# Block products with fewer multiplications for the last quarter of a feed-forward's first matmul, with token and weight sums made on chip

## The chip, the cores and the metric

One core of one Trainium2 chip runs the whole program. The metric is the device time of one execution in microseconds. TensorE multiplies, VectorE (DVE), ScalarE (ACT) and GpSimd (POOL) do elementwise work, SyncE (SP) issues the loads.

## The reference

Three layers in a row, all in float32. The first is a linear recurrence over 768 steps for 2 batches of 8 heads of 48. Its result, 1536 tokens of 384, goes through a feed-forward with ELU, and that through four experts with ReLU, weighted by shares.

```python
x = attn_out.transpose(0, 2, 1, 3).reshape(1536, 384)
h = x @ w_in                                              # 384 -> 2048
g = np.where(h > 0.0, h, np.exp(np.minimum(h, 0.0)) - 1.0)
x = g @ w_out                                             # 2048 -> 384
p = domain_probs / (domain_probs.sum(-1, keepdims=True) + 1e-09)
for e in range(4):                                        # 384 -> 1024 -> 384 each
    out += p[:, e:e + 1] * (np.maximum(x @ w1[e], 0.0) @ w2[e])
```

## The kernel before

**Numbers.** A float32 operand is kept as a rounded high part and the rest, its low part, and a product is three matmuls (high by high, high by low, low by high) into one PSUM bank (`PASSES`). ScalarE makes high parts (`copy("A", ...)`, L192), VectorE or GpSimd low parts (`sub`, L188). Weights of the first feed-forward come as float64 words and are turned into both parts by `piece`: `wl` loads, `wa`, `wb` and `wc` convert (L219 to L261). Tokens are 3 blocks of 512, features 128 to a block; a matmul is 128x128 by 128x512.

**First feed-forward.** `step(n)` has n = 12 q + 4 bl + f: quarter q of the 2048 hidden features, token block bl, feature block f in the quarter. `h` is the hidden product, 9 matmuls (L478) and two activations for the ELU; `e` the rest of the ELU on VectorE (L486) and the high part; `el` the low part; `z` nine matmuls into three PSUM banks (L505), which collect four f; `dr` adds the banks into `x2` (L514), and in the last quarter splits the new x into high (ScalarE) and low (GpSimd).

**Second feed-forward, `experts`.** Two feature blocks by three token blocks by three parts of the inner dimension are a *unit*. The first two units are plain products (`plain`, L709: 36 of 3 matmuls, 12 banks, copied out by `plain_taken` on ScalarE). The other fourteen are made of 15 block products instead of 18 (`product`, L677): sums of token blocks (`sum_tokens`, L657, split by `tokens_hi` and `tokens_lo`, L660 to L667) by sums of weight blocks (`sum_blocks` on GpSimd, L595, split by `split_hi` and `split_lo`), collected in five chains of banks and drained by `taken` (L689 to L696: 10 on VectorE, 5 on ScalarE). `second` (L738) are the second products, of hidden low parts made at L731.

**What sets the order.** All is under a manual schedule: each engine runs its instructions in the order in which the program writes them. For attention and the first feed-forward that order is the string `ORDER`, tokens such as `h20`, `el20D` (step and engine: A ScalarE, D VectorE, P GpSimd). The part behind `|` overlaps with `experts`: each token gets a key that counts 3 for an h or a z and ends at -1 with the last, and the events of `experts` have keys in rows of one block product, row 0 being the first plain product.

```python
            n -= 3 * (token[0] in "hz")
...
            at(n - (75 if u > 2 else 112 if u == 2 else 95), load_blocks, u)
...
            at(made[t[0]], sum_tokens, t[0] in FIRST, *t)
```

So unit 2's blocks are loaded 70 rows ahead of row 0, summed from 55 and split from 40 rows ahead; the first 16 token sums have the keys -0.9 to 14.85, and the hidden low parts that the first second products read have 12.7 to 17.2. Buffers that matter: two for `blocks`, three for `sums` (split weights), two for `e`, three for `hl`, eight PSUM banks.

## Time and profile before

| | |
|---|---|
| median of 3 runs | 644.77 us (643.35 to 647.09) |
| the profiled execution's own time | 641.47 us |
| its span | 639.7 us |
| granted TensorE clock | 0.997 of full speed |
| TensorE busy | 627.2 us, 98% |
| VectorE busy | 485.2 us, 76% |
| GpSimd busy | 363.1 us, 57% |
| ScalarE busy | 302.0 us, 47% |

The span is the profiled execution from its first to its last instruction; the own time is a little longer. The profile and the runs are different executions. Line numbers (L677) are those of the kernel before.

### The profile page before, as it was taken

How to read it: one execution, taken by the hardware profiler on the slowest of the kernel's cores; microseconds unless marked ns; L12 is line 12 of the kernel's file. 1: busy time of each engine (PE TensorE's matmuls, PEld its weight loads, DVE VectorE, ACT ScalarE, POOL GpSimd, SP SyncE). 2: the span in 40 equal slices, each digit the busy share in tenths (PEclk: the TensorE clock that was granted, in tenths of full speed). 3: DMA queues.
4: the chain of work that ended last, by engine and by line, in shares of the span. 5: the costliest groups of instructions: out<-in, count | busy, mean ns of one | idle time of the engine just before them, and what ended most of it. 6: DMA issues, size and time to landing. Idle time of an engine off the chain costs nothing.

```text
span 639.7 us, 10184 instructions
## 1 busy us (share of the span) xinstructions
PE 627.2 (98%) x3858; PEld 513.2 (80%) x3858; DVE 485.2 (76%) x709; ACT 302.0 (47%) x587; POOL 363.1 (57%) x320
## 2 busy tenths in 40 slices
PE   9999999999999999999999999999999999999995
PEld 7777878788888888888888888888888888888884
DVE  7899995537759633598876987977978968878683
ACT  2666755456757636557434424433532434344230
POOL 6876465103232538648452876876876867754252
PEclk9999999999999999999999999999999999999998
DMA  8966640131231300003103112012220121400012
GB/s 317 344 225 206 209 167 9 46 123 50 75 99 37 138 1 0 1 0 115 51 18 108 41 34 91 26 45 81 70 79 18 41 75 33 124 1 1 0 50 105
DMA packets 20974, 52.07 MB, mean 81 GB/s; under 512 B 2680, under 2 KB 3880, under 8 KB 20916
## 3 DMA queue, kind: packets, MB, share of 16 engines
q1 hardware_dynamic: 20772, 51.33, 24.2%
q8 instruction: 32, 0.52, 0.4%
q14 instruction: 26, 0.21, 0.1%
q10 hardware_dynamic: 144, 0.00, 0.0%
HBM read 47.76 MB, written 2.38 MB: 78 GB/s over the span
## 4 chain that ended last, share of the span: by engine, by line
PE 90%; DVE 5%; DMA 3%; issue 1%; ACT 0%; SPq 0%; DVEq 0%; ACTq 0%
PE second L738 29%; PE bank L505 14%; PE bank L478 14%; PE chain_a L677 9%; PE chain_b L677 6%; PE chain_p L709 4%; PE chain_c L677 3%; PE chain_d L677 3%; DMA v<-in_vv 2%; PE chain_e L677 1%; PE bank L138 1%; DMA raw<-in_w_out 1%; PE bank L361 1%; PE bank L368 1%; DVE t L224 1%
## 5 line engine op out<-in xcount | busy, mean ns | idle before, releaser
L738 PE MATMUL second<-hl,w2s 128*128 128x512 f32 x864 | 230.8, 389 | 0.1
L738 PEld LDWEIGHTS second<-hl,w2s 128*128 128x128 f32 x864 | 162.0, 188 | 34.3 <-DVE hl L188 0.5
L756 POOL TENSOR_TENSOR x<-scaled,x 128x512 f32<-128x512 f32 x60 | 84.1, 1420 | 91.5 <-DVE scaled L748 91.3
L478 PE MATMUL bank<-x,w 128*128 128x512 f32 x432 | 105.1, 391 | 0.0
L505 PE MATMUL bank<-hl,w 128*128 128x512 f32 x432 | 104.8, 391 | 0.0
L731 DVE SCALAR_TENSOR_TENSOR hl<-terms,hl 128x512 fp32r<-128x512 f32 x92 | 95.1, 1046 | 11.0 <-ACT hl L725 11.0
L505 PEld LDWEIGHTS bank<-hl,w 128*128 128x128 f32 x432 | 80.7, 188 | 17.1 <-issue 0.3
L478 PEld LDWEIGHTS bank<-x,w 128*128 128x128 f32 x432 | 80.6, 188 | 17.1 <-issue 0.3
L188 POOL TENSOR_TENSOR sums<-blocks,sums 128x512 fp32r<-128x512 f32 (+1 forms) x56 | 74.8, 1345 | 26.9 <-ACT sums L192 26.9
L188 POOL TENSOR_TENSOR hl<-e,hl 128x512 fp32r<-128x512 f32 x26 | 35.6, 1372 | 74.0 <-ACT hl L192 74.0
L595 POOL TENSOR_TENSOR blocks<-blocks 128x256 f32<-128x256 f32 x84 | 73.5, 893 | 1.2 <-DMA blocks<-in_w 0.5
L486 DVE SCALAR_TENSOR_TENSOR e<-e,bank 128x512 f32<-128x512 f32 x48 | 32.6, 681 | 50.7 <-ACT e L482 50.7
L692 ACT ACTIVATE terms<-chain_b 128x512 f32<-128x512 f32 x28 | 16.8, 600 | 106.0 <-PE chain_b L677 106.0
L725 ACT ACTIVATE hl<-terms 128x512 fp32r<-128x512 f32 x96 | 58.1, 624 | 14.1 <-PE second L738 6.8
L692 ACT ACTIVATE terms<-chain_a 128x512 f32<-128x512 f32 x28 | 16.8, 598 | 77.3 <-PE chain_a L677 77.3
L481 ACT ACTIVATE e<-bank 128x512 f32<-128x512 f32 x48 | 28.6, 595 | 48.6 <-PE bank L478 45.5
L677 PE MATMUL chain_a<-x,sums 128*128 128x512 f32 x168 | 47.3, 390 | 0.0
L748 DVE TENSOR_TENSOR scaled<-second,pr 128x512 f32<-128x512 f32 x60 | 40.6, 686 | 2.7 <-PE second L738 1.4
L230 POOL TENSOR_TENSOR raw<-raw,t 128x384 int32<-128x384 int32 x21 | 22.2, 1063 | 31.6 <-ACT t L226 24.2
L689 DVE TENSOR_TENSOR terms<-terms,chain_a 128x512 f32<-128x512 f32 x42 | 28.7, 682 | 14.0 <-PE chain_a L677 13.4
L192 ACT ACTIVATE hl<-e 128x512 fp32r<-128x512 f32 x48 | 30.0, 627 | 15.8 <-DVE e L486 10.9
L677 PEld LDWEIGHTS chain_a<-x,sums 128*128 128x128 f32 x168 | 31.5, 188 | 6.9 <-DVE terms L689 0.4
(129 smaller groups left out, 966.9 us busy)
## 6 DMA issues: line engine op xcount, KB each, us to landing
v<-in_vv SPq DMA_DIRECT2D x12, 544.0 KB, 6.1
kr<-in_wkr SPq DMA_DIRECT2D x12, 512.0 KB, 5.7
raw<-in_w_out SPq DMA_DIRECT2D x16, 384.0 KB, 3.5
raw<-in_w_in SPq DMA_DIRECT2D x16, 384.0 KB, 4.5
blocks<-in_w SPq DMA_DIRECT2D x16, 384.0 KB, 3.3
raw<-in_w SPq DMA_DIRECT2D x16, 384.0 KB, 4.3
w<-in_wkr SPq DMA_DIRECT2D x12, 262.5 KB, 5.5
gw<-in_wkr SPq DMA_DIRECT2D x12, 262.0 KB, 2.8
```

Of the source, the lines that this page charges most:

```text
L188: engines[e].tensor_tensor(o, a, b.bitcast(F32), ALU.subtract)
L478: nc.tensor.matmul(ph, lhsT=wi[:, sa, f, kk, :], rhs=x[:, kk, c0:c0 + nch, sm], start=(kk == 0 and i == 0), stop=(kk == 2 and i == 2))
L486: nc.vector.scalar_tensor_tensor(b["e"], b["e"], -1.0, b["ph"], ALU.add, ALU.max)
L505: nc.tensor.matmul(pxs[q, bl][d][:, :cols], lhsT=wo[:, sa, f, d * P:(d + 1) * P], rhs=b["t"][:, sm], start=(f == 0 and i == 0), stop=(f == ...
L595: nc.gpsimd.tensor_tensor(*(places(blocks[u], p) for p in (r, a, c)), ALU.subtract if op == "-" else ALU.add)
L677: nc.tensor.matmul(banks[c], lhsT=weights(u, r, sa), rhs=tokens(r)[:, sm], start=r in HEADS and i == 0, stop=i == 2, skip_group_check=True)
L692: nc.scalar.activation(out=new({0: 0, 6: 5, 3: 2, 5: 3, 8: 4}[r]), in_=ps, func=AF.Copy, scale=-1.0 if r in (6, 8) else 1.0)
L725: nc.scalar.activation(out=hls[f, b][:, 0], in_=results[f, b], func=AF.Copy if weighted else AF.Relu)
L731: nc.vector.scalar_tensor_tensor(hls[f, b][:, 1], results[f, b], 0.0, hls[f, b][:, 0].bitcast(F32), ALU.max, ALU.subtract)
L738: nc.tensor.matmul(sums[d], lhsT=w[:, sa, f, d * P:(d + 1) * P], rhs=hls[4 * h + f, b][:, sm], start=f == i == 0, stop=f == 3 and i == 2)
L748: nc.vector.tensor_tensor(o, sums[d], prs[h // 2, b], ALU.mult)
L756: nc.gpsimd.tensor_tensor(x2[:, d, s], scaled[d], x2[:, d, s], ALU.add)
```

## The change

The last quarter's hidden products (h36 to h47) are made by two more units of 15 block products, numbered -2 and -1, inside the lead. Products are tokens p0 to p29 and their drains k0 to k29. The quarter's weights are laid out as blocks; `wb12` to `wb15` round into the `blocks` buffers, and `sb` (sums) and `sp` (splits) make the operands. Token blocks are put together again from high and low part and summed by 25 `pt` tokens, split by 12 `tf` tokens into places of x that are no longer read. `x` starts the ELU from a finished sum in SBUF (two activations), `y` is the rest of it on VectorE, then `e`, `el` and `z` as before; five of the z are cut in three (`za`, `zb`, `zc`). Results of unit -2 lie in the quarter's weight buffer, those of unit -1 among the eight `first` buffers, which are now handed out one by one. Because units -2 and -1 use the two `blocks` buffers, loads and splits of units 0 and 1 and of unit 2's first part move to tokens (`mb`, `mu`, `ms`) near the end of the order, with unit 2's sums on VectorE instead of GpSimd.

```diff
+GROUPS = {"h": 3, "z": 3, "za": 1, "zb": 1, "zc": 1, "p": 1}
...
+PARTS = [((1, 1), None, None), ((2, 1), None, None), ("q", (1, 1), (2, 1)), ((1, 0), None, None), (8, (1, 0), (1, 1)),
+         ((2, 0), None, None), ("s2", (2, 0), (2, 1)), ("v", 8, "s2"), (12, 8, (2, 1)), ((0, 1), None, None),
...
+z7 e18 e17 el18P z16 dr7A h19 xd11 | el17D pt3D pt12D pt0D pt9D pt1D pt13P z17 e19 h8 pt5D pt4D pt6D z18 el19D pt2P
+pt8D pt14P tf8P e8 tf12D h11 e11 z19 el8D dr19D h9 e9 el11D pt10P h10 wl8 z8 pt11D el9D e10 el10D pt7P tf11D h20 wl9
+z9 wa9D wa8D e20 h21 wb9D wl11 wb8D pt15D el20D wa11D wc9D z10 pt19D h22 wl10 z11 wc8P e21 wl24 wa10D e22 wb11D wl25
+wb10D el22D wc11D tf1D el21D wc10D pt22D wl27 tf0D dr11A h23 wl26 wa24D z20 pt16P h24 e23 wb24D wa25D z21 el23D wc24D
+pt21D e24 wb25P h25 z22 pt17D wa27D wl12 el24D e25 h27 wb27P wa26D el25D wc25P wb26P z23 wl13 e27 dr23D h26 pt20P
+wa12D z24 el27D wc26P e26 wa13D h28 z25 tf4P el26D wb12D wl15 wb13D h29 wc27D e28 sb0D z26 e29 el28D h30 z27 wl28 wl14
+pt23D el29D wa15D e30 wl29 wb15D dr27D sb1P tf7P el30D h32 z28 sp0D h31 wa14D wb14P tf10P z29 pt18D e32 e31 wl31 p0
+z30 k0 p1 el31D tf13D sb2D k1 p2 k2 sp1D h33 p3 el32D z31 k3 p4 pt24P tf9P e33 k4 el33D tf5D h34 p5 wa28D k5 e34 h35
+sb3P p6 dr31D wb28P k6 p7 tf2D mb0 z32 el34P k7 p8 k8 wl30 sp2P p9 k9 x36 za33 p10 e35 p11 zb33 zc33 k10 k11 wa30D p12
+k12 y36 p13 p14 x37 wa29D p15 e36 p16 za34 k13 k14 p17 el35D k15 k16 k17 zb34 y37 wc28P x40 sp3P wb29D el36D p18 p19
+wa31D wb30D k18 k19 zc34 p20 za35 y40 p21 k20 wc29P k21 zb35 zc35 p22 p23 e37 e40 dr35D k22 wb31P za36 k23 p24 el40P
+x41 k24 p25 zb36 k25 p26 x38 y41 el37P p27 wc30P k26 zc36 mb1 y38 p28 wc31P za37 k27 k28 x39 e38 y39 x45 zb37 zc37 e39
+z40 el38D x42 e41 y45 el39D z38 y42 el41P x44 z39 x43 y44 z41 e44 y43 p29 x46 el44P e42 el42P e45 dr39D z44 y46 el45D
+e46 z42 k29 el46D x47 e43 el43D y47 z45 e47 z46 el47D mu0D z43 mb2 ms2D mu1D z47 mu2P dr43D dr47D
...
+            if key == 3 and fifteen:
+                u = q // 2 - 2
+                if u not in blocks:
+                    blocks[u] = pools["blocks"].tile([P, 17, P], F32, tag="blocks", name="blocks")
+                at = 6 + 3 * (q % 2)
+                engines[e].tensor_tensor(blocks[u][:, at:at + 3].rearrange("q b c -> q (b c)").bitcast(I32), hi, b["t"], ALU.add)
+                return
...
+        def summed():
+            b["ph"] = results[f - 4, bl]
+            started()
+
+        def joined():
+            nc.vector.scalar_tensor_tensor(b["ph"], b["e"], -1.0, b["ph"], ALU.add, ALU.max)
+            b["e"] = b["ph"]
...
+            if (f - 4, bl) in held:
+                released((f - 4, bl))
...
-        def sum_blocks(u, r, a, op, c):
-            nc.gpsimd.tensor_tensor(*(places(blocks[u], p) for p in (r, a, c)), ALU.subtract if op == "-" else ALU.add)
+        def sum_blocks(u, r, a, op, c, e="P"):
+            engines[e].tensor_tensor(*(places(blocks[u], p) for p in (r, a, c)), ALU.subtract if op == "-" else ALU.add)
...
+        def sum_parts(e, name, a, c):
+            t = full["m", name] = kept(("m", name))
+            if a is None:
+                k, i = name
+                hi, lo = (x[:, k, 4 * i:4 * i + 4, m].bitcast(F32) for m in range(2))
+                engines[e].tensor_tensor(t.rearrange("q (n c) -> q n c", n=4), hi, lo, ALU.add)
+            else:
+                engines[e].tensor_tensor(t, full["m", a], full["m", c], ALU.add)
+                used(("m", a), ("m", c))
...
-                results[2 * u + o // 3, o % 3] = term()
+                f, b = 2 * u + o // 3, o % 3
+                results[f, b] = term() if u >= 0 else kept((f, b)) if u == -1 else wt64[3].rearrange(
+                    "p s (n c) -> p (s n) c", c=512)[:, o].bitcast(F32)
...
-            n -= 3 * (token[0] in "hz")
+            n -= GROUPS.get(token.rstrip("0123456789"), 0)
...
+        def sum_tokens_of(n, e):
+            sum_parts(e, *PARTS[n])
+
+        def split_tokens(r, e):
+            tokens_hi(r, ("m", r))
+            tokens_lo(e, r, ("m", r))
+
+        def sum_weights(n, e):
+            for t in SUMS[3 * (n % 2):3 * (n % 2) + 3]:
+                sum_blocks(n // 2 - 2, *t, e)
+
+        def split_weights(u, part, e):
+            for i in (0, 4):
+                m = min(4, 8 - part - i)
+                split_hi(u, part, (9, 0)[part], 8 - part, i, m)
+                split_lo(e, u, part, (9, 0)[part], 8 - part, i, m)
+
+        def split_first(u, e):
+            if u == 2:
+                return split_weights(u, 0, e)
+            for i in (0, 3):
+                split_hi(u, 0, 6, 6, i, 3)
+                split_lo(e, u, 0, 6, 6, i, 3)
+
+        def sum_first(u, e):
+            for t in SUMS:
+                sum_blocks(u, *t, e)
+
+        if lead:
+            fifteen.update(p=lambda n: product(n // 15 - 2, TURNS[n % 15]), k=lambda n: taken(n // 15 - 2, TURNS[n % 15]), pt=sum_tokens_of,
+                           tf=split_tokens, sb=sum_weights, sp=lambda n, e: split_weights(n // 2 - 2, n % 2, e), mb=load_blocks,
+                           mu=split_first, ms=sum_first)
         for u in range(16):
             n = place["product", u, 0] if u > 1 else -90 + 12 * u
+            if lead and u < 3:
+                if u == 2:
+                    for i in (0, 4):
+                        at(n - 10 + i, split_hi, u, 1, 0, 7, i, min(4, 7 - i))
+                        at(n - 8.6 + i, split_lo, "P", u, 1, 0, 7, i, min(4, 7 - i))
+                continue
```

Before the bar the order is the same. The host also lays out the last quarter of `w_in` by blocks; the loads keep their sizes. The tail of the order before reads `e46 h47 el46P dr43D z44 e47 el47D z45 z46 z47 dr47D`.

## Rows read from the trace of the kernel before

**Rows 1.** The page's totals: busy us (share of the span) and instructions of each engine.
```profile
PE 627.2 (98%) x3858; PEld 513.2 (80%) x3858; DVE 485.2 (76%) x709; ACT 302.0 (47%) x587; POOL 363.1 (57%) x320
```

**Rows 2.** The chain that ended last, in order: start us, us, what.
```profile
260.55 8.16 PE bank L505 x36
268.71 24.48 PE chain_p L709 x108
```

**Rows 3.** Windows by stage: length, then busy us of each engine, clock, DMA.
```profile
132.03:200.00 67.97, 67.97 (x301) 56.30 (x301) 43.83 (x76) 44.61 (x80) 17.99 (x16) 1.00 0.22 65
200.00:268.55 68.55, 68.55 (x305) 56.76 (x303) 34.84 (x53) 38.18 (x68) 36.87 (x32) 1.00 0.11 36
268.55:293.03 24.48, 24.48 (x110) 20.28 (x108) 24.38 (x28) 14.03 (x28) 14.66 (x11) 1.00 0.00 1
```

**Rows 4.** Timeline of VectorE, operations back to back: start us, us, engine, line.
```profile
168.93 0.55 DVE L188 TENSOR_TENSOR w<-raw,w 128x384 fp32r<-128x384 f32 x1
169.40 0.68 DVE L486 SCALAR_TENSOR_TENSOR e<-e,bank 128x512 f32<-128x512 f32 x1
...
258.53 1.88 DVE L514 TENSOR_TENSOR x<-bank,x 128x512 f32<-128x512 f32 x3
...
303.59 0.68 DVE L748 TENSOR_TENSOR x<-second,pr 128x512 f32<-128x512 f32 x1
304.19 0.67 DVE L689 TENSOR_TENSOR terms<-terms,chain_a 128x512 f32<-128x512 f32 x1
304.79 0.68 DVE L748 TENSOR_TENSOR x<-second,pr 128x512 f32<-128x512 f32 x1
```

**Rows 5.** Groups by line and shape in the window 124 to 268.3.
```profile
L230 POOL TENSOR_TENSOR raw<-raw,t 128x384 int32<-128x384 int32 x10 | 10.5, 1067 | 19.0 <-ACT t L226 11.6 <-issue 7.4
...
L595 POOL TENSOR_TENSOR blocks<-blocks 128x256 f32<-128x256 f32 x5 | 4.1, 826 | 0.1
L188 POOL TENSOR_TENSOR sums<-blocks,sums 128x512 fp32r<-128x512 f32 x2 | 2.6, 1282 | 0.0
...
L595 POOL TENSOR_TENSOR blocks<-blocks 128x128 f32<-128x128 f32 x1 | 0.5, 459 | 0.0
```

**Rows 6.** The tile blocks: its loads' time from issue to landing.
```profile
DMA to landing us min/median/max: 3.0/3.3/5.5
```

**Rows 7.** Timeline of VectorE at the start and near the end of the plain stretch.
```profile
267.39 2.05 DVE L514 TENSOR_TENSOR x<-bank,x 128x512 f32<-128x512 f32 x3 [1.79 <-PE bank L505]
269.36 1.31 DVE L657 TENSOR_TENSOR first<-x 128x512 f32<-128x512 f32 x1
270.59 1.64 DVE L188 TENSOR_TENSOR w2s<-raw,w2s 128x384 fp32r<-128x384 f32 x1
272.15 1.78 DVE L657 TENSOR_TENSOR first<-first,x 128x512 f32<-128x512 f32 x1
...
295.11 1.28 DVE L731 SCALAR_TENSOR_TENSOR hl<-terms,hl 128x512 fp32r<-128x512 f32 x2
```

**Rows 8.** Timeline of GpSimd: low parts of hidden products and of the new x.
```profile
258.43 2.55 POOL L188 TENSOR_TENSOR hl<-e,hl 128x512 fp32r<-128x512 f32 x2 [3.40 <-ACT hl L192]
...
268.82 4.56 POOL L188 TENSOR_TENSOR x<-x,x 128x512 fp32r<-128x512 f32 x3 [2.08 <-ACT x L192]
```

**Rows 9.** Timeline of ScalarE near the end of the plain stretch.
```profile
290.30 0.63 ACT L660 ACTIVATE xb<-first 128x512 fp32r<-128x512 f32 x1 [1.18 <-DVE first L657]
290.84 1.14 ACT L725 ACTIVATE hl<-terms 128x512 fp32r<-128x512 f32 x2
291.88 1.55 ACT L192 ACTIVATE terms<-chain_p 128x512 f32<-128x512 f32 x3
```

**Rows 10.** Timeline of TensorE where the second products begin.
```profile
293.03 4.24 PE L738 MATMUL second<-hl,w2s 128*128 128x512 f32 x18
297.11 0.84 PE L677 MATMUL chain_b<-x,sums 128*128 128x512 f32 x3
297.79 0.84 PE L738 MATMUL second<-hl,w2s 128*128 128x512 f32 x3
```

More of the change, by code (lines that the diff above doesn't have):

```diff
@@ L206, in kernel_body, with kept, released @@
     wt64 = {}
+    blocks, parted, results, fifteen = {}, {}, {}, {}
+    places_free, held = deque(range(8)), {}
+    def kept(name, t="first"):
+        held[name] = places_free.popleft()
+        return pools["first"].tile([P, 512], F32, tag=f"first{held[name]}", name=t)
+    def released(name):
+        places_free.append(held.pop(name))
     def piece(n):
@@ L520, in sums @@
                     sub("P", lo, new, hi)
-        return {"h": hidden, "e": elu, "el": elu_lo, "z": second, "dr": sums}
+        return {"h": hidden, "x": summed, "y": joined, "za": lambda: second((0,)), "zb": lambda: second((1,)),
+                "zc": lambda: second((2,)), "e": elu, "el": elu_lo, "z": second, "dr": sums}
     work = {}
@@ L655, in of, with used, tokens_hi, tokens_lo @@
                 return x2[:, i[0], 512 * i[1]:512 * i[1] + 512] if isinstance(i, tuple) else full[i]
[L656 removed]
+            full[name] = kept(name) if early else term()
             nc.vector.tensor_tensor(full[name], of(a), of(c), ALU.add)
[L659 to L662 removed]
+            used(a, c)
+        def sum_parts(e, name, a, c):
[7 more added lines that the diff above has]
+                used(("m", a), ("m", c))
+        uses = {}
+        for name, a, c in TOKENS:
+            for n in (a, c):
+                uses[n] = uses.get(n, 0) + 1
+        for name, a, c in PARTS:
+            for n in (a, c):
+                uses["m", n] = uses.get(("m", n), 0) + 1
+        for r in PLACE:
+            uses[r] = uses.get(r, 0) + 1
+            uses["m", r] = uses.get(("m", r), 0) + 1
+        def used(*names):
+            for n in names:
+                if n in held:
+                    uses[n] -= 1
+                    if not uses[n]:
+                        released(n)
+        def tokens_hi(r, name=None):
+            nc.scalar.activation(out=tokens(r)[:, 0], in_=full[name or r], func=AF.Copy, scale=-1.0 if r in MINUS else 1.0)
+        def tokens_lo(e, r, name=None):
             hi, lo = (tokens(r)[:, m] for m in range(2))
+            t = full[name or r]
             if r in MINUS:
[L665 removed]
+                nc.vector.scalar_tensor_tensor(lo, t, -1.0, hi.bitcast(F32), ALU.mult, ALU.subtract)
             else:
[L667 to L670 removed]
+                sub(e, lo, t, hi)
+            used(name or r)
+        banks = {}
         def product(u, r):
@@ L942, in kernel_body @@
                 recur(i, gp, u_turned)
-        work.clear()
+        for t in (work, fifteen, held):
+            t.clear()
+        places_free.clear()
+        places_free.extend(range(8))
         bank_pool(m0, 8)
```

90 lines of the change are left out of this document (42 added, 48 removed), and 3 rows, old and new, of the table PARTS.

## The prediction

> **What bounds the kernel now.** I read the engine totals first: TensorE is busy for 98% of the span and VectorE for 76% [rows 1]. The chain of work that ended last, read in order of time, then says whether that matters here: in the stretch that the change touches it is one unbroken run of matmuls, the last 36 of the first feed-forward and then 108 plain products, at 24.48/108 = 0.227 us each [rows 2]. So a matmul less is 0.227 us less, as long as TensorE goes on being fed. The windows by stage say who feeds it [rows 3]. In what I call the lead (132.03, where the order written after the bar begins, to 268.55, 136.5 us) VectorE has 43.8 + 34.8 = 78.7 us of work and GpSimd 18.0 + 36.9 = 54.9. In the plain stretch behind it (268.55 to 293.03) VectorE has 24.38 us of work in 24.48: no room at all. That is the number the reader should keep: whatever makes VectorE late at the start of the plain stretch is still there at its end.
>
> **The change part by part: TensorE.** Twelve hidden products of 9 matmuls (108) become two units of 15 products of 3 (90). The z steps that are cut in three keep their matmuls. So 18 matmuls go: 18 x 0.227 = 4.08 us, and the lead shrinks to 132.4 us if nothing waits.
>
> **What VectorE and GpSimd get in the lead.** Back to back, a VectorE operation on 512 columns starts every 0.60 us and one on 384 every 0.47 [rows 4]. By the tokens of the new order VectorE gains 11 low parts that GpSimd had, 17 token sums, 7 token splits, 20 of the 30 drains and 4 weight splits: 59 x 0.60 = 35.4 us. Twelve block sums on VectorE (11 of 256 columns, 1 of 128) have no row; the step from 384 to 512 columns is 0.13 us, which gives 0.34 and 0.21, so 4.0 us as an estimate. The weight pieces change by one operation less, -0.5. Sum 38.9, so 117.6 of 132.4 us: 89% where it was 58%. GpSimd loses 11 low parts (14.2), gains 17 operations of 1.29 (21.9) and six block sums (4.2), and loses the third unit's sums and first split and three net weight operations (10.3) [rows 5]: 56.5 us. ScalarE had 82.8 us [rows 3] and gains about 30 activations, some 16 us: it stays far from full. The twelve y replace twelve e one for one. All this fits under the matmuls, so I cost it at nothing; what hides it is the distance from each h to its z, some 10 us in the new order (between h33 and za33 stand seven products, two z and two h, 12.9 us). From below it can give nothing back, since TensorE doesn't wait in this stretch now; from above it is the price of rival two.
>
> **What is late at the end of the lead.** Here I do find a price. The third unit's blocks used to be loaded and summed on GpSimd long before; now their load stands behind the first unit's split (two block buffers), and both stand behind the last hidden products. I follow that chain from the end of product p29, which lies six z steps, 54 matmuls or 12.24 us, before the plain stretch. VectorE drains p29 (0.7). ScalarE has three copies and e46 ahead of x47, until 1.2, and x47 is two activations of 0.63: 2.5. Then e43 (3.1), el43 on VectorE (3.8), y47 (4.4; 4.9 with GpSimd's splits of block 0 in the way), e47 and el47 (6.2), the split of unit 0 in two pieces of 384 (7.2). Only now may the load go: 3.3 us to landing [rows 6], 10.6. Then, in VectorE's queue, ms2 (six sums, 1.9: 12.5), mu1 (two pieces, 1.0: 13.5), and behind them the six sums into x2 of the last two token blocks (3.6: 17.1). That is 17.1 - 12.24 = 4.9 us into the plain stretch. Before, VectorE began the next work, the first token sum, 0.81 us into it (269.36) [rows 7]. So it starts 4.1 us later into a stretch that is full.
>
> **What contention adds.** With two operands in SBUF, VectorE shares time with GpSimd: GpSimd's three x splits from 268.82 took 4.56 us and exactly three VectorE operations came through beside them [rows 7, 8], 1.52 us a pair, so each GpSimd operation costs VectorE 1.52 - 0.60 = 0.92 us. An operation that reads PSUM isn't touched: three in 1.88 us while GpSimd ran two [rows 4, 8]. Before, about 2.6 of those splits still lay ahead when VectorE began its token sums; after the change it is five, because unit 2's weight split goes ahead of the x splits of blocks 1 and 2 on GpSimd. 2.4 x 0.92 = 2.2 us more. VectorE is then 4.1 + 2.2 = 6.3 us late.
>
> The Trainium skill (SBUF — State Buffer, "SBUF: two separate sides") says that VectorE and GpSimd share a port pair by an exclusive lock, and that the loser "fully blocks" for the other's whole instruction. By that each of the 2.4 would cost VectorE a whole 1.29 us instead of 0.92, VectorE would be 7.2 us late, and the sum below would come out 0.9 us longer; rows 7 show 0.92, and I take the rows.
>
> **Who waits for it.** ScalarE's copies of the plain products free their PSUM banks, and they stand in its queue behind token copies that wait for VectorE's sums. There are eight banks; twelve plain products and three second sums claim fifteen. The 14th claim, the second sum's second bank at 293.03 + 0.68 = 293.71, needs the sixth copy freed; that is the first of the three from 291.88 (held until then behind a copy that waited for VectorE at 290.30), done at 292.46 [rows 9, 10]. The cushion is 1.25 us. The next one is the low part of the third hidden block: done at 295.79, wanted at 298.0, cushion 2.2 [rows 7, 10]. So TensorE waits 6.3 - 1.25 = 5.1 us there.
>
> **The sum.** -4.08 + 5.1 = +1.0 us. Against the profiled execution's own time, 641.47 (span 639.7 and 1.8 around it), 642.5; the three timed runs lie higher, median 644.77, so on that scale 645.8. From below: load at its shortest (3.0), no added contention, a wait of 2.55, net -1.5: 643.3. From above: load at its longest (5.5 [rows 6], +2.2) gives a wait of 7.3, net +3.2: 648.0.
>
> **Rivals.** *One: the matmuls' gain is kept* (-4.1, 640.7). The wait would have to be under 0.9 us, so VectorE no more than 2.1 us late. For it: TensorE waits nowhere in the lead or the plain stretch now, and the bank claims are read by me from their count, not from a wait that the trace shows. Against: the chain from p29 is long whatever its pieces measure, and VectorE has 0.1 us idle to catch up in. 17%.
>
> *Two: the port pair becomes the bound of the lead*, slower. Of VectorE's 117.6 us, 65 operations read PSUM (21 e, 20 drains, 24 sums), 39 us; the other 78.6 and GpSimd's 56.5 make 135 us if each holds the pair alone, against 132.4 of matmuls: at least 2.7 us of wait on top, 3.3 to take a middle. At the rows' 0.92 for 1.29 it is 78.6 + 40.3 = 119, and fits; before it was 99 of 136.5. It would show first ahead of p0, where el30 and the first unit's split stand some 4 us ahead of their users. Net +4.3: 649.1. It decides from a wait of 2.2 us in the lead. 20%.
>
> Rival two is the exclusive lock that the Trainium skill states (SBUF — State Buffer, "SBUF: two separate sides"), at full strength; by 0.92 of 1.29 us the trace bears it out in part, and its chance is set by that.
>
> *Three: the tail alone is late enough*, with the load near its longest and lower splits blocked: +3.5, 648.3. 8%.
>
> **How the numbers follow.** Half a per cent, 3.2 us, is about what a measurement of this kernel can tell from no change. The forecast, -1.5 to +3.2 around +1.0, has 55% and is "same"; rival one is faster (17%); rivals two and three slower (28%). I predict 645.8, range 640.6 to 649.5: it reaches to rival one below and past the middle of rival two above. The forecast's own range is 643.3 to 648.0.
>
> **What would show it.** 3840 matmuls instead of 3858 (324 hidden ones, 720 block products). VectorE idle for some 3 us until the third unit's blocks land, just ahead of the plain stretch; the first token sum 4 to 6 us into that stretch; a wait of TensorE of about 5 us at the end of the plain products, released by ScalarE's copies or VectorE's low parts; none over 1 us in the lead. The prediction is wrong if TensorE runs through the start of the second products without a wait, or if waits of more than 2 us stand between p0 and p29.

## The result, and the profile after

The changed kernel takes 648.86 us (median of 11 runs, 647.24 to 653.20), the kernel before 644.57 (11 runs beside it, 641.05 to 647.09). The ratio is 1.0081, 95% interval 1.0054 to 1.0108: **0.8% slower**. The profiled execution took 649.5 us, with a span of 647.8.

The totals of the page and its line of TensorE's granted clock (40 slices, tenths of full speed):

```profile
PE 626.7 (97%) x3840; PEld 510.9 (79%) x3840; DVE 532.5 (82%) x779; ACT 315.2 (49%) x613; POOL 371.3 (57%) x323
PEclk9999999999999999997999999999999999999999
```

The 18 matmuls are gone (3840 for 3858 in [rows 1]), and VectorE has 47 us more. One slice of the clock line, the 19th (291.5 to 307.7 us), is lower than the others. Line numbers in the rows below are those of the kernel whose row it is; they differ from those of the kernel before. Now the stages, each from the start of a TensorE row: the first z17 matmul (131.87 before, 132.49 after), the first plain product (268.55, 265.51), the first pair product `chain_b` (297.11, 304.07), the matmul `chain_n` near the end (619.62, 626.55), the span's end (639.7, 647.8).

| stage | before | after | difference |
|---|---|---|---|
| lead, from that z17 on | 136.68 | 133.02 | -3.66 |
| plain products and first second products | 28.56 | 38.56 | +10.00 |
| pairs, to `chain_n` | 322.51 | 322.48 | -0.03 |
| end | 20.08 | 21.25 | +1.17 |

The rest of the 8.1 us between the two spans, 0.6, lies ahead of z17, where the order is the same. So the saving arrives, and one stage of 28 us takes back nearly three times as much. The timeline of TensorE there (start us, us, engine, line, operation, out<-in, count; in brackets what it waited for):

```profile
265.51 4.24 PE L794 MATMUL chain_p<-x,sums 128*128 128x512 f32 x18
270.48 16.59 PE L794 MATMUL chain_p<-x,sums 128*128 128x512 f32 x72 [0.73 <-DVE x L562]
287.82 4.39 PE L794 MATMUL chain_p<-x,sums 128*128 128x512 f32 x18 [0.76 <-ACT terms L203]
294.67 0.98 PE L823 MATMUL second<-hl,w2s 128*128 128x512 f32 x3 [2.46 <-ACT terms L203]
297.98 6.25 PE L823 MATMUL second<-hl,w2s 128*128 128x512 f32 x15 [2.33 <-ACT terms L203]
304.07 0.86 PE L760 MATMUL chain_b<-x,sums 128*128 128x512 f32 x3
```

Two things are to be seen. There are four waits: the first for the late sums into x2 (L562), the other three for ScalarE's copies of the plain products (`terms`, L203). And the 15 matmuls from 297.98 need 6.1 us to the next row, where 15 x 0.227 = 3.4 would do. In the kernel before, the first of [rows 10] has no wait: 18 matmuls in 4.1 us. The windows of the same stretch (length, busy us of PE, PEld, DVE, ACT, POOL, then the clock) say why the matmuls got longer:

```profile
265.50:291.90 26.40, 24.92 (x109) 19.93 (x107) 25.90 (x35) 12.60 (x24) 15.71 (x11) 1.00 0.05 15
291.90:304.07 12.17, 7.37 (x21) 5.30 (x20) 12.17 (x13) 10.10 (x20) 9.56 (x9) 0.72 0.16 56
296.70:297.98 1.28, 0.00 (x0) 0.00 (x1) 1.28 (x3) 1.28 (x4) 1.28 (x2) 0.50 0.00 0
297.98:303.50 5.52, 5.52 (x13) 4.37 (x14) 5.52 (x8) 5.52 (x12) 2.99 (x3) 0.50 0.25 82
303.50:304.07 0.57, 0.57 (x4) 0.45 (x4) 0.57 (x2) 0.36 (x1) 0.57 (x2) 1.00 1.03 395
```

The mean granted clock is 0.72 in the second. The last three windows cut its end finer: the clock was at the lower of TensorE's two levels (0.50, that is 1.2 of 2.4 GHz) from 296.7, in the last wait, to 303.5, when the matmuls had been running again for 5.5 us. So the 10.0 us are 2.7 us of lower clock (6.1 - 3.4) and about 7.3 us of waits. (The four brackets add up to 6.28. They count from the modelled end of the matmul before, which is 0.16 us after the next could have started, and the first matmuls behind a wait are a little slower.) The second window also has VectorE busy for all of its 12.17 us. Upstream of it, VectorE's timeline around the start of the plain stretch at 265.51:

```profile
252.11 1.77 DVE L526 SCALAR_TENSOR_TENSOR first<-e,first 128x512 f32<-128x512 f32 x1
253.80 0.68 DVE L199 TENSOR_TENSOR hl<-w,hl 128x512 fp32r<-128x512 f32 x1
254.41 0.67 DVE L774 TENSOR_TENSOR first<-first,chain_c 128x512 f32<-128x512 f32 x1
256.22 1.22 DVE L199 TENSOR_TENSOR hl<-first,hl 128x512 fp32r<-128x512 f32 x1 [1.14 <-ACT hl L203]
...
261.11 1.02 DVE L199 TENSOR_TENSOR sums<-blocks,sums 128x384 fp32r<-128x384 f32 x2
265.60 2.10 DVE L646 TENSOR_TENSOR blocks<-blocks 128x256 f32<-128x256 f32 x6 [3.47 <-DMA blocks<-in_w]
267.61 2.12 DVE L199 TENSOR_TENSOR sums<-blocks,sums 128x384 fp32r<-128x384 f32 x2
269.65 3.67 DVE L562 TENSOR_TENSOR x<-bank,x 128x512 f32<-128x512 f32 x6
273.24 0.93 DVE L708 TENSOR_TENSOR first<-x 128x512 f32<-128x512 f32 x1
```

The last drain of a block product (L774) ends 1.65 us after p29's matmuls; unit 0's split (261.11) ends at 262.13; VectorE stands 3.47 us for the load; the first token sum (L708) starts at 273.24, 7.7 us into the plain stretch, where it was 0.81 before [rows 7]. At the far end of the stretch, ScalarE:

```profile
295.78 0.63 ACT L741 ACTIVATE xb<-first 128x512 fp32r<-128x512 f32 x1 [1.16 <-DVE first L708]
296.31 1.13 ACT L810 ACTIVATE hl<-terms 128x512 fp32r<-128x512 f32 x2
297.35 1.55 ACT L203 ACTIVATE terms<-chain_p 128x512 f32<-128x512 f32 x3
```

These are the three rows of [rows 9], 5.5 us later by the clock and 8.5 us later counted from the start of the plain stretch. The sum that ScalarE waits for ended at 290.27 before and at 295.75 after. I call this **the deciding sum** below: it is the last token sum that a split ahead of those copies waits for.

### The profile page after: what moved, and what is told of

Same layout as the page of the kernel before. It is cut to its first block, busy times and chain, and to the rows that moved or that the text cites. A ratio compares the mean times of both kernels' runs of the same rounds, so it can differ in the third digit from the quotient of the medians.

```text
span 647.8 us, 10257 instructions
## 1 busy us (share of the span) xinstructions
PE 626.7 (97%) x3840; PEld 510.9 (79%) x3840; DVE 532.5 (82%) x779; ACT 315.2 (49%) x613; POOL 371.3 (57%) x323
## 4 chain that ended last, share of the span: by engine, by line
PE 84%; DVE 9%; DMA 3%; issue 2%; ACT 1%; SPq 0%; DVEq 0%; ACTq 0%
PE second L823 29%; PE bank L553 13%; PE bank L511 10%; PE chain_a L760 10%; PE chain_b L760 7%; PE chain_c L760 3%; PE chain_d L760 3%; DMA v<-in_vv 2%; PE chain_e L760 2%; PE bank L149 1%; DVE first L708 1%; PE bank L390 1%; DVE terms L708 1%; DMA x<-x 1%; PE bank L397 1%
## 5 line engine op out<-in xcount | busy, mean ns | idle before, releaser
L199 POOL TENSOR_TENSOR sums<-blocks,sums 128x512 fp32r<-128x512 f32 (+1 forms) x60 | 80.5, 1354 | 47.2 <-ACT sums L203 47.2
L816 DVE SCALAR_TENSOR_TENSOR hl<-terms,hl 128x512 fp32r<-128x512 f32 x92 | 95.0, 1045 | 12.6 <-ACT hl L810 12.6
L511 PE MATMUL bank<-x,w 128*128 128x512 f32 x324 | 79.6, 392 | 0.2 <-DVE am L196 0.2
L646 POOL TENSOR_TENSOR blocks<-blocks 128x256 f32<-128x256 f32 (+1 forms) x84 | 73.7, 895 | 1.8 <-DVE blocks L646 0.7
L511 PEld LDWEIGHTS bank<-x,w 128*128 128x128 f32 x324 | 60.3, 188 | 13.2 <-DVE am L196 0.4
L760 PE MATMUL chain_a<-x,sums 128*128 128x512 f32 x192 | 54.0, 390 | 0.0
L203 ACT ACTIVATE sums<-blocks 128x512 fp32r<-128x512 f32 (+1 forms) x68 | 39.4, 593 | 6.5 <-DVE blocks L646 5.1
L760 PE MATMUL chain_b<-x,sums 128*128 128x512 f32 x144 | 40.9, 392 | 0.0
L774 DVE TENSOR_TENSOR terms<-terms,chain_a 128x512 f32<-128x512 f32 x42 | 28.7, 683 | 14.3 <-PE chain_a L760 13.7
L518 ACT ACTIVATE e<-bank 128x512 f32<-128x512 f32 x36 | 21.4, 595 | 29.0 <-PE bank L511 29.0
L259 POOL TENSOR_TENSOR raw<-raw,t 128x384 int32<-128x384 int32 x16 | 17.0, 1060 | 30.9 <-ACT t L248 30.9
L760 PEld LDWEIGHTS chain_b<-x,sums 128*128 128x128 f32 x144 | 26.6, 188 | 6.4 <-DVE terms L774 1.1
```

Of the source, the lines that this page charges most:

```text
L199: engines[e].tensor_tensor(o, a, b.bitcast(F32), ALU.subtract)
L203: nc.scalar.activation(out=o, in_=a, func=AF.Copy)
L511: nc.tensor.matmul(ph, lhsT=wi[:, sa, place(kk)], rhs=x[:, kk, c0:c0 + nch, sm], start=(kk == 0 and i == 0), stop=(kk == 2 and i == 2))
L646: engines[e].tensor_tensor(*(places(blocks[u], p) for p in (r, a, c)), ALU.subtract if op == "-" else ALU.add)
L760: nc.tensor.matmul(banks[c], lhsT=weights(u, r, sa), rhs=tokens(r)[:, sm], start=r in HEADS and i == 0, stop=i == 2, skip_group_check=True)
L816: nc.vector.scalar_tensor_tensor(hls[f, b][:, 1], results[f, b], 0.0, hls[f, b][:, 0].bitcast(F32), ALU.max, ALU.subtract)
```

## The experiments

Seventeen runs of sixteen kernels were made, each ratio against the kernel before on the same chip. The theory to be tested is the forecast's: the tail (load, sums and splits of the third unit's blocks behind the last hidden products) makes VectorE late, VectorE makes ScalarE's copies late, the copies hold PSUM banks, and TensorE waits. The rivals are that VectorE and GpSimd contend for their port so much that the place of the load doesn't matter, and that the lead itself has become too tight.

**The load early.** Unit 0's split and the two loads go ahead into the product stretch; `ms2` to `mu2` stay.

```diff
-el36D p18 ... zc34 p20 ... zc36 mb1 ... el47D mu0D z43 mb2 ms2D mu1D z47
+el36D mu0D p18 ... zc34 mb1 mb2 p20 ... zc36 ... el47D z43 ms2D mu1D z47
```

> Order alone: unit 0's split (mu0D) moves to behind el36D and the loads of units 1 and 2 (mb1, mb2) to behind zc34, so unit 2's blocks land some 25 us before they are wanted; its sums (ms2D) and unit 1's split (mu1D) stay on VectorE where they were, ahead of the last sums into x2. Theory 'late load' (VectorE stands 3.5 us for the landing, and all behind it is late): VectorE's first token sum comes some 2.4 us into the plain stretch instead of 7.7, about 1.6 us later than in the kernel before; with GpSimd's extra splits it is some 4 us late at the second products, TensorE waits some 3 us there instead of 7.3 and its clock doesn't fall; time 0.5 to 2 us under the kernel before. Rival 'port pair in the plain stretch' (the work moved there is the cost, not the wait): TensorE still waits 5 us or more and the time stays 3 to 5 us above before. Rival 'the units cost it in the lead': nothing changes, 5 us above before.

Measured: 1.0152 (1.0103 to 1.0201), worse than the change. Two lines of its timelines, VectorE and TensorE:

```profile
232.49 1.82 DVE L199 TENSOR_TENSOR sums<-blocks,sums 128x384 fp32r<-128x384 f32 x2 [2.88 <-ACT sums L203]
```
```profile
237.91 1.65 PE L760 MATMUL chain_a<-x,sums 128*128 128x512 f32 x3 [4.98 <-DVE first L774]
```

VectorE stood 2.88 us at `mu0` for ScalarE. The drains of two products are queued behind it, and the next product of a chain waits for its drain: 4.98 us. The granted clock fell in that wait too (0.50 from 237.91 to 243.50), and the lead came out 7.9 us longer than the change's 133.0. So VectorE has no room for a piece with a wait in that stretch. The wait at the second products was one of 2.36 us, much less than in the changed kernel, so the load does count, but moving it has to keep clear of the drains.

**The same, clear of the drains.** Unit 0's split goes to GpSimd, behind `wc31P` near the end of the products, and the third load behind it.

```diff
-wc31P za37 ... el47D mu0D z43 mb2 ms2D mu1D z47 mu2P
+wc31P mu0P mb2 za37 ... el47D z43 ms2D mu1D z47 mu2P
```

> The load alone again, without touching VectorE in the stretch of the block products: unit 0's split goes to GpSimd (mu0P) behind wc31P, where GpSimd stands idle, and the load of unit 2 (mb2) behind it; unit 2's sums, unit 1's split and unit 2's first split stay in the tail, in front of the last sums into x2. No wait of TensorE between p0 and p29. 'Late load' and 'queue and port pair' together: the 3.5 us of standing for the landing go, the sums and splits stay, so VectorE's first token sum comes 2 to 3 us into the plain stretch (7.7 in the changed kernel, 0.8 in the one before), GpSimd's x splits end some 4 to 5 us later than before, VectorE is 4 to 4.5 us late at the second products and TensorE waits about 3 us: time 0 to 1.5 us under the kernel before. Rival 'the load's landing is all of it': TensorE waits under 1 us and the time is 3 to 4 us under before. Rival 'the landing is nothing': 4 to 6 us above before as the changed kernel.

Measured: 0.9991 (0.9971 to 1.0012), no wait from p0 to p29, and one wait at the second products, of 2.37 us. The whole 0.8% is back with a load moved and a split given to another engine.

**The tail alone.** The kernel before with all of its hidden products and none of the block products of units -2 and -1, but with the changed kernel's tail.

```diff
-z36 z35 ... h40 z38 ... z46 z47 dr47D
+z36 mb0 z35 ... h40 mb1 z38 ... z46 mu0D mb2 ms2D mu1D z47 mu2P dr47D
```

> The kernel before with the moved tail alone: no units -2 and -1, the last quarter's twelve hidden products as before, but loads, sums and splits of units 0 to 2 at the end of the order as in the change (mb0 and mb1 earlier, mu0D, mb2, ms2D, mu1D, mu2P behind the last hidden products). 'Late load': VectorE waits some 3.5 us for the landing, the last sums into x2 end some 6 us into the plain stretch, TensorE waits 5 to 8 us there and at the second products; time 5 to 10 us above before. Rival 'the units cost it in the lead': no more than 1 us above before.

Measured: 1.0118 (1.0089 to 1.0147). The tail alone costs 7.1 us by the medians, with nothing saved for it, and the same waits stand at the same rows (1.41 and 2.35 us before the second products, for ScalarE's copies), with one of 1.53 for unit 1's split. In its profiled execution the lead takes 136.68 us, as before, and the stage from the first plain product to `chain_b` 7.8 us more. This settles that the loss is the tail's and not that of the block products.

**The third unit's sums and last split on GpSimd, behind the x splits.**

```diff
-z43 mb2 ms2D mu1D z47 mu2P dr43D dr47D
+z43 mb2 mu1D z47 dr43D dr47D ms2P mu2P
```

> Order alone: the load of unit 2 stays late, but VectorE doesn't wait for it: its sums go to GpSimd (ms2P) and with its first split (mu2P) behind the last sums into x2 and their splits. Theory 'late load': VectorE's first token sum comes about 1 to 2 us into the plain stretch, TensorE's wait at the second products falls from 7.3 to under 3 us, time near or under before. Rival 'port pair in the plain stretch': GpSimd now has some 7 us more work there (six sums, two splits), which costs VectorE 0.6 to 0.9 us each; VectorE is 6 to 8 us late at the second products, TensorE waits 5 to 6 us, time 2 to 5 us above before.

Measured: 1.0072 (1.0047 to 1.0098). VectorE's first token sum started at 266.28, 1.1 us into the plain stretch, and then:

```profile
276.65 1.15 DVE L199 TENSOR_TENSOR w2s<-raw,w2s 128x384 fp32r<-128x384 f32 x1 [9.43 <-ACT w2s L203]
```

ScalarE's queue stood behind the high copies of `mu2`, which waited 8.02 us for GpSimd's sums, and these stood behind GpSimd's six x splits (264.12 to 272.13). The time lies where the rival said, but not for its reason: VectorE stood, it didn't share. The wait had only moved to another queue, and this run tells the theories apart no further.

**All of it early, and two places for the sums.** The first takes every step of the tail forward; the other three keep the load where the run clear of the drains had it, and put `ms2`, `mu2` and `mu1` into gaps of VectorE further ahead.

```diff
+el36D mu0D ... zc34 mb1 mb2 ... k24 mu1D ... dr39D ms2P ... el47D mu2P z43 z47 dr43D dr47D   (all early)
+wc31P mu0P mb2 ... el46D ms2D ... e47 mu2P ... el47D mu1D   (sums behind el46)
+wc31P mu0P mb2 ... y43 ms2D ... e43 mu2P ... el47D mu1D     (sums behind y43)
+wc31P mu0P mb2 ... y42 ms2D ... e43 mu2P ... el47D mu1D     (sums behind y42)
```

> Order alone: loads early as in the first run, and also unit 2's sums on GpSimd behind the third last sum into x2 (where GpSimd stands idle for 9 us), unit 1's split behind k24 and unit 2's first split behind el47D. Nothing of units 0 to 2 is left ahead of the last sums into x2. Both 'late load' and 'port pair in the plain stretch': VectorE's first token sum within 1.5 us of the plain stretch's start, TensorE waits under 1 us at the second products, no fall of its clock; time 3 to 4 us under the kernel before (ratio 0.994 to 0.9955) and 8 to 9 us under the changed one. Rival 'the units cost it in the lead': waits appear between p0 and p29 and the time stays at or above before.

> Order alone: as the other run of this call, and unit 2's sums on VectorE behind el46D, its first split on GpSimd behind e47, unit 1's split behind el47D, so that nothing of units 0 to 2 stands between the last z and the last sums into x2 on any engine. If the tail's load, queue and port pair are the whole of the loss: first token sum within 1.2 us of the plain stretch's start, GpSimd's six x splits end 1.5 to 2 us later than before, VectorE 1 to 1.5 us late at the second products, TensorE's wait there under 0.5 us, clock full; the time is 3 to 4 us under the kernel before, ratio 0.994 to 0.9955. Rival 'the units cost it anywhere': other waits take the place, time at or above before.

> The run before it left VectorE's chain from p29 to the last sums as long as it was (unit 2's sums and unit 1's split, 3.2 and 2.4 us, stood in it). Here unit 2's sums stand ahead of that chain, behind y43, its first split on GpSimd behind e43, and only unit 1's split is left between el47 and the last sums, with its high parts no longer behind other copies on ScalarE. Theory 'the chain from p29 is too long for the 12.2 us of matmuls behind it': first token sum within 1.5 us of the plain stretch's start, GpSimd's x splits end 1.5 to 2.5 us later than before, TensorE waits 0 to 1 us at the second products, full clock; 2.5 to 4 us under the kernel before, ratio 0.9935 to 0.996. Rival 'whatever is put into the lead costs it there': a wait appears among the last z instead, time within 1 us of before.

> The same, with unit 2's sums one step earlier still, behind y42, where VectorE stands for 1.2 us anyway: the load has 1 to 2 us less time to land. Same theory: the same 2.5 to 4 us under before, or 1 us less if y44's delay reaches z44.

Measured: 1.0148 (1.0117 to 1.0179), 1.0002 (0.9984 to 1.0019), 1.0017 (0.9989 to 1.0045) and 0.9992 (0.9964 to 1.0020). The gain that I expected of the last three did not come. With the sums behind y43 there are new waits among the last z (1.16, 0.33 and 0.18 us) and the lead is 2.6 us longer than the change's, so there the rival of that run is right in part. All early pays 5.0 and 1.7 us at drains in the lead, as the first run did. But it shows one thing cleanly: its first token sum started 0.81 us into the plain stretch, exactly as before the change, and still the deciding sum ended 3.7 us late and TensorE waited 2.29 us. GpSimd's row says why; the second line is the changed kernel's:

```profile
274.93 9.65 POOL L199 TENSOR_TENSOR x<-x,x 128x512 fp32r<-128x512 f32 x6
```
```profile
271.07 9.22 POOL L199 TENSOR_TENSOR x<-x,x 128x512 fp32r<-128x512 f32 x6 [0.21 <-ACT x L203]
```

Six low parts of the new x (9.2 us and more) now lie beside the first token sums, where there were three (4.56) [rows 8]: z43 has become the last but one step of TensorE in the order, so that the splits of two token blocks come at once. That is the second part of the lateness, and no place of the load takes it away.

The versions agree on its size. When the first token sum starts, 2.6 splits are still ahead before the change, 4.3 in the change and in the five other versions with the load early, and 6.0 in all early. From there to the deciding sum VectorE loses 1.6 to 1.7 us with 4.3 of them and 3.7 us with 6.0, counted against the kernel before: 0.9 to 1.1 us for each split more. The tail alone is the check. Its order leaves three splits behind the first token sum (2.7 ahead):

```profile
277.84 4.56 POOL L195 TENSOR_TENSOR x<-x,x 128x512 fp32r<-128x512 f32 x3 [0.20 <-ACT x L199]
```

Its first token sum is 7.1 us late, later than the change's, and its deciding sum 7.2: only 0.15 us came on top.

**The rule of the waits.** The eleven late versions that leave ScalarE's order as it is (two of them come from the next paragraph) can now be laid side by side. "Late" is the end of the deciding sum counted from the first plain product, less the 21.72 us of the kernel before; "extra" is the time from there to `chain_b`, less 28.56; "slow" is what the 15 second matmuls took beyond the 3.71 of the rows at full clock.

| version | late | extra | slow | extra - slow | late - 1.25 |
|---|---|---|---|---|---|
| the change | 8.52 | 10.00 | 2.54 | 7.46 | 7.27 |
| sums on GpSimd behind | 8.85 | 9.97 | 2.19 | 7.78 | 7.60 |
| block sums of unit 3 later (next paragraph) | 8.00 | 8.38 | 1.43 | 6.95 | 6.75 |
| tail alone | 7.24 | 7.77 | 1.59 | 6.18 | 5.99 |
| sums behind el46 | 5.18 | 6.71 | 2.58 | 4.13 | 3.93 |
| load early, clear of the drains | 4.09 | 4.56 | 1.53 | 3.03 | 2.84 |
| load early | 4.07 | 4.62 | 1.60 | 3.02 | 2.82 |
| all early | 3.67 | 2.62 | 0.01 | 2.61 | 2.42 |
| sums behind y42 | 3.60 | 4.13 | 1.59 | 2.54 | 2.35 |
| sums behind y43 | 3.30 | 2.25 | 0.00 | 2.25 | 2.05 |
| sums behind y42, unit 3 later | 2.45 | 1.39 | 0.00 | 1.39 | 1.20 |

The cushion of 1.25 us that the forecast read from the bank claims is 0.2 us too large in all eleven alike: what the rows show, "late" less "extra - slow", is 1.05 to 1.07 us every time. What the forecast got wrong is mainly the lateness that goes in, and the clock.

**Contention taken out.** GpSimd sums unit 3's blocks in the last third of the plain stretch (287.39 to 294.04 before, 292.88 to 299.5 after). They are needed some 25 us later, so they can go behind the first second products.

```diff
-at(n - (50 if u > 2 else 97) + 2 * i, sum_blocks, u, *s)
+at(n - 31 + 1.3 * i if lead and u == 3 else n - (50 if u > 2 else 97) + 2 * i, sum_blocks, u, *s)
-(0, 9, 8, n - (34 if u > 2 else 82))
+(0, 9, 8, n - (24 if lead and u == 3 else 34 if u > 2 else 82))
```

> The changed kernel with one thing moved: GpSimd's six block sums of unit 3, which stand in the last third of the plain stretch (292.88 to 299.5) beside some nine full VectorE instructions that each take 1.2 instead of 0.68 us, come after the first second products. Theory (TensorE waits because VectorE's token sums are late, and part of that lateness is VectorE waiting for GpSimd): the last token sum ends 4 to 4.5 us earlier, so the wait of about 7.3 us shrinks to about 3 us, and the clock loss of 2.7 us stays or shrinks: 642 to 645 us, ratio to the kernel before 0.997 to 1.002. Rival (the late load alone sets it, the shared port costs nothing): no change from the changed kernel, ratio 1.007 to 1.009.

> Control: the kernel before with the same move of unit 3's six block sums. TensorE waits nowhere in the plain stretch of the kernel before, so there is nothing to win by earlier token sums: both theories expect ratio 0.999 to 1.001. If unit 3's sums are then too late for its first products, a wait at unit 3's start would show and the ratio go above 1.002.

> The version with load, sums and splits pulled ahead into free gaps (its one wait 2.23 us before the second products and some 1.8 us of lower clock behind it), with unit 3's six block sums behind the first second products as well. Theory: the token sums end about 4 us earlier, the wait of 2.23 us and the clock loss go, and the 3.6 us of the saved matmuls are kept: 640 us, ratio 0.993 to 0.996. Rival (the port costs nothing): ratio 0.998 to 1.000 as without the move.

Measured: 1.0061 (1.0040 to 1.0082), 0.9988 (0.9966 to 1.0009) and 0.9983 (0.9954 to 1.0011). VectorE's same instruction in the changed kernel and in the first of these:

```profile
294.53 1.22 DVE L708 TENSOR_TENSOR first<-first,x 128x512 f32<-128x512 f32 x1
```
```profile
294.23 0.68 DVE L708 TENSOR_TENSOR first<-first,x 128x512 f32<-128x512 f32 x1
```

Beside a block sum of GpSimd it takes 1.22 us, without one 0.68: 0.54 us each. My expectation counted all nine such instructions. Only two of them count, the deciding sum itself (this row) and one ahead of it: 1.1 us, of which this run's longer stand for the load (4.01 us for 3.47) took half back. The sum came 0.5 us less late, and not 4. In the version with its sums behind y42 the move took the wait from 2.23 to 1.09 and the lower clock with it, and that version's profiled span was 638.4 us. Contention with the block sums is a term, and a small one.

**ScalarE's order.** ScalarE's copies stand behind the splits of three combinations (`xb`) that are first read some 10 us into the pairs. Here these splits go behind the last copy.

```diff
-k = max(made[r] + 0.7, {0: 11.5, 1: 23.5, 2: 35.5}[n % 3] + 0.9 * (n // 3) if n < 9 else -99)
+k = max(made[r] + 0.7, {0: 11.5, 1: 23.5, 2: 35.5}[n % 3] + 0.9 * (n // 3) if n < 9
+        else 37 + 0.9 * (n - 12) if n > 11 and lead else -99)
```

> The changed kernel with one thing moved: the high and low parts of the three token combinations that are needed last (the three in xb, first read by a product some 10 us into the pairs) are made behind ScalarE's last copy of the plain products instead of ahead of four of them. No instruction is added. Theory (TensorE waits for banks, because ScalarE's copies stand in its queue behind splits that wait for late token sums): ScalarE no longer stands for these sums (1.3 and 0.7 us in the rows), the waits fall by 2 to 4 of the 7.3 us and the clock loss at most stays: ratio to the kernel before 1.001 to 1.005. Rival (the lateness of VectorE alone sets the time, whatever stands ahead of the copies): 1.007 to 1.009.

> Control: the kernel before with the same move. TensorE has no wait there, so both theories expect 0.999 to 1.001.

> The version with load, sums and splits pulled ahead and unit 3's block sums moved back (one wait of 1.09 us left before the second products), with this move too. Theory: the last wait goes (under 0.2 us left) and nothing else changes: about 1 us less than that version, ratio 0.994 to 0.998, faster than the kernel before beyond its interval. Rival (something else holds the banks): the wait stays near 1.1 us and the ratio at 0.998 to 0.999.

Measured: 1.0157 (1.0130 to 1.0184), 1.0054 (1.0033 to 1.0074) and **0.9954 (0.9931 to 0.9978)**. The third, the sums behind y42 with both moves, is called the best version below. The first two missed badly. TensorE in the changed kernel with this move:

```profile
296.21 2.33 PE L823 MATMUL second<-hl,w2s 128*128 128x512 f32 x9 [1.55 <-DVE hl L816]
299.43 2.11 PE L823 MATMUL second<-hl,w2s 128*128 128x512 f32 x8 [0.89 <-DVE hl L816]
306.43 0.96 PE L760 MATMUL chain_d<-x,sums 128*128 128x512 f32 x3 [0.64 <-ACT terms L777]
314.78 1.65 PE L760 MATMUL chain_a<-x,sums 128*128 128x512 f32 x3 [3.96 <-DVE terms L774]
```

The waits for copies at the second products are gone, so it was the banks. But VectorE is still 9.4 us late. What comes next in its queue is now what TensorE waits for: the low parts of the hidden blocks (L816), then the drains of the pairs (L774). The drain behind the 3.96 us stands in VectorE's queue behind a load, that of the shares `pr`:

```profile
306.53 3.48 DVE L747 SCALAR_TENSOR_TENSOR xb<-first,xb 128x512 fp32r<-128x512 f32 x2
310.16 1.28 SPq L696 DMA_DIRECT2D pr<-rows  x3
313.44 0.69 DVE L833 TENSOR_TENSOR x<-second,pr 128x512 f32<-128x512 f32 x1 [2.23 <-DMA pr<-rows]
314.05 0.68 DVE L774 TENSOR_TENSOR terms<-terms,chain_a 128x512 f32<-128x512 f32 x1
```

The pool of `pr` opens when that of the `first` buffers closes, and the `xb` splits that I moved are the last to read `first`; the profile puts SyncE's wait ahead of this load down to them. They end at 310.01, the load goes out at 310.16, and VectorE stands 2.23 us for it: more than half of the 3.96. In the kernel before with this move it is the whole: the splits end at 302.66, the load goes out at 302.81, VectorE stands 2.47 us, and TensorE waits 1.91 at a drain. So the moved work did not only stand ahead of a drain; it held up a load. A move to a place where "there is time" on TensorE's side had run into both.

**Both moves together**, and the best version once more:

> The changed kernel, its tail as it is, with both moves: unit 3's block sums behind the first second products, and the splits of the three combinations needed last behind ScalarE's copies. Theory (banks are freed late by ScalarE's queue, and behind that VectorE itself is late with the hidden layer's low parts and the drains of the pairs; GpSimd's block sums cost it 2.7 us there): no wait on copies at the second products beyond 0.3 us; of the 2.4 and 4.0 us that TensorE waited for VectorE with the second move alone, 1 to 3 us are left: ratio 0.999 to 1.004. Rival (the late load makes the loss whatever is moved behind it): 1.006 or more.

> Control: the kernel before with both moves. Alone the second move cost it 1.9 us of wait at a chain's drain, behind VectorE pieces that took longer beside GpSimd's block sums; with the first move as well that should be gone: ratio 0.998 to 1.002. If the gain of the best version came from the two moves and not from the 18 matmuls, this would be 0.994 to 0.997.

> The best version (load, sums and splits pulled ahead, both moves) once more beside this control on the same chip: 0.993 to 0.998, and at least 1.5 us below the control, if the 18 matmuls that the change saves are what is gained; equal to the control, if the moves are.

Measured, on one chip: the changed kernel with both moves 1.0030 (1.0010 to 1.0050), 645.67 us; the kernel before with both 1.0014 (0.9993 to 1.0035), 644.06 us; the best version 0.9960 (0.9942 to 0.9979), 641.39 us, after 0.9954 the first time. The moves give the kernel before nothing, so the best version's gain is not theirs: 2.7 us below its control, of the 3.66 that the lead saves. Its plain stretch in the first of its two runs, two rows of TensorE without any wait:

```profile
264.88 24.64 PE L794 MATMUL chain_p<-x,sums 128*128 128x512 f32 x108
289.36 4.24 PE L823 MATMUL second<-hl,w2s 128*128 128x512 f32 x18
```

From the first plain product to `chain_b` it takes 28.56 us, as the kernel before did. The changed kernel with both moves still pays 2.36 us there and 2.35 at a drain behind it:

```profile
307.08 1.18 PE L760 MATMUL chain_a<-x,sums 128*128 128x512 f32 x3 [2.35 <-DVE terms L774]
```

At that drain VectorE stood 1.88 us for the load of `pr`, which again went out when the `xb` splits ended (302.13). They end so late because the third unit's load is late: the first token sum started 6.8 us into the stretch. It needs that load early as well, and then the change keeps most of what its matmuls save.

## Why the prediction was wrong

The forecast was "same", 645.8 us, with the forecast's own range to 648.0; it came out slower by 0.8%, at 648.86. Its mechanism was right, one of its sizes, the lateness at the first token sum, was 2.8 us too small, and one term was missing. That 648.86 lies in the outer range (640.6 to 649.5) and near rival two's 649.1 is chance: rival two's mechanism did not happen.

**Right.** The 18 matmuls went, and the lead shortened by 3.66 us of the forecast 4.08 (most of the missing 0.4 lies between 216.8 and 221.3, where matmuls came slower without a wait). VectorE was busy for 115.9 us of it and GpSimd for 55.5 (forecast 117.6 and 56.5). TensorE waits nowhere between p0 and p29, so rival two, the port pair as the bound of the lead, falls, for the order as it was written. The runs with the load early show how little room it has: one VectorE piece with a wait among the drains costs a wait of 5 us, and with the lower clock behind it 7.9. The path of the loss (late load, VectorE, ScalarE's copies, banks) is the one forecast, and the cushion of 1.25 us was 0.2 too large in eleven versions.

**The step that failed: "What is late at the end of the lead".** It put the first token sum 4.9 us into the plain stretch; it was 7.7. Piece by piece, counted from p29's end at about 253.4:

| end of | forecast | measured | step's share of the error |
|---|---|---|---|
| k29 | 0.7 | 1.65 | +0.95 |
| mu0 | 7.2 | 8.7 | +0.55 |
| load landed | 10.6 | 12.2 | +0.1 |
| ms2 | 12.5 | 14.3 | +0.2 |
| mu1 | 13.5 | 16.3 | +1.0 |
| six x2 sums | 17.1 | 19.9 | 0 |

The load, which I gave the widest bound, was 3.44 us (forecast 3.3). The two large errors are VectorE instructions that I costed alone though GpSimd was at work beside them: y46, two places ahead of k29 in VectorE's queue, took 1.77 us where the one at 259.06 took 0.68, and the two pieces of `mu1` took 2.12 where the two of `mu0`, with GpSimd idle, took 1.02. I had a price for that from [rows 7, 8] and used it only inside the plain stretch.

**What contention adds** was forecast at 2.2 us. The deciding sum came 8.5 us late, and 7.7 - 0.8 = 6.9 us of this were there at the first token sum, so 1.6 came on top. The price of 0.92 us for each split was about right and the count was not: I took five splits as still ahead, and 4.3 were, 1.7 more than before, and 1.7 x 0.92 = 1.6. The Trainium skill (SBUF — State Buffer, "SBUF: two separate sides") says that of two such instructions the loser "fully blocks" for the whole of the other's. The trace agrees only in part: beside a block sum of 0.83 us [rows 5] VectorE lost 0.54, as it lost 0.92 of 1.29 beside a split. That the six splits are the place is shown by the comparison of the versions above, three splits in the tail alone and six in the others; no run changed their number and nothing else.

**The missing term.** In the last of the waits TensorE's granted clock fell, and the 15 matmuls behind it took 2.5 to 2.7 us more. The forecast had no such term. The three add up: -3.66 + 7.3 + 2.7 = +6.3 us in the profiled execution, where the medians say +4.3 and the ratio +5.2. The kernel before was profiled in an execution 3.1 us under its median, so the profiled difference is the larger. The profiled run's remaining 1.8 us lie ahead of z17 and in the end stage, and no experiment was made for them.

**Rival three**, the tail alone late enough, named the outcome but not its reason: it wanted the load near its longest, and the load was of ordinary length.

## What to carry to other kernels

When matmuls are saved by work on other engines, look for the price at the seam, where the next stage's loads and splits were displaced. Lay the chain out from the last instruction that can't move, each VectorE piece at its price beside GpSimd where GpSimd is busy, and compare its end with the place where the old kernel began. A queue in order makes a wait out of whatever stands ahead: before moving work "to where there is time", ask in every queue that it enters what stands behind it there, and which load waits for the buffer that it reads. Four of the moves here only handed the wait on, to a drain, a copy, a low part or a load. And a wait that is only partly shortened can leave nothing to see: 0.9983 with 1.1 us of it left can't be told from no change, 0.9954 without it can, though the two intervals overlap.

## What the hardware showed that was not expected

The granted clock fell to its lower level around waits of 2.2 to 2.5 us, in a stretch that is otherwise full. In the rows of the eleven versions the 15 second matmuls that follow a wait take 3.71 us or 5.1 to 6.3; over these rows alone the mean granted clock is 1.00 for the first and 0.56 to 0.70 for the others. Three rows, from the version with its sums behind y43, from that with its sums behind y42, and from all early:

```profile
294.74 3.71 PE L823 MATMUL second<-hl,w2s 128*128 128x512 f32 x15 [1.94 <-ACT terms L203]
```
```profile
293.17 5.30 PE L823 MATMUL second<-hl,w2s 128*128 128x512 f32 x15 [2.23 <-ACT terms L203]
```
```profile
301.73 3.72 PE L823 MATMUL second<-hl,w2s 128*128 128x512 f32 x15 [2.29 <-ACT terms L203]
```

A wait of 2.23 us was followed by the lower level and one of 2.29 by the higher, so the length of the wait alone doesn't decide. The Trainium skill (TensorE: Matmul & The Clock Gate, "Part 1: The HAM clock gate (the "warmup" mystery)") says of the rise of the clock at a kernel's start that it is "run-variable". These rows are of a fall in the middle of a kernel, and with one profile of most kernels no run here shows whether it varies in the same way. For a forecast: of the nine versions in the table with a wait of 2.2 us or more, eight lost another 1.4 to 2.6 us to the lower clock behind it, and one lost nothing.
